# A two-layer network after window attention on one core: its second layer by Strassen's scheme, with decoded weights and activations kept in DRAM

## The chip, the cores and the metric

The kernel runs on one core of a Trainium2 chip. The metric is the device time of one execution in microseconds (us). The core has a matrix engine (PE, also called TensorE; its weight loads are listed as PEld), a vector engine (DVE), a scalar engine (ACT), GpSimd (POOL) and an engine that issues transfers (SP). They share an on-chip memory, SBUF; PE writes its sums to accumulators in PSUM.

## The reference

```python
# q, k, v: (4, 8, 576, 64) fp32; weights fp64
scores = where(0 <= i - j < 64, scale * q @ k.T, -1e9)
attn = softmax(scores)                               # attn @ v: 2304 tokens x 512
x = (attn @ v).transpose(0, 2, 1, 3).reshape(2304, 512)
h = maximum(maximum(x @ w1, x @ w2), x @ w3)         # 512 -> 768
x = h @ w_out                                        # 768 -> 512
h = x @ w_in                                         # 512 -> 2048
g = where(h >= 1, h, where(h <= -1, 0, (h + 1) ** 2 / 4))
out = g @ w_out2                                     # 2048 -> 512
```

## The kernel before

Three pieces of work follow one another and overlap. The attention runs in 36 groups of 64 queries (all 8 heads at once). The first layer runs in 9 blocks of 256 tokens: 18 products (6 tiles of 128 features by 3 weights, `a_item`) whose maximum is taken as they are read out of PSUM, the tiles `ht`, and 4 products back to 512 features (`b_item`). Its results `x2s` go to DRAM (`x2d`). The second layer runs in blocks of 512, 512, 512, 512 and 256 tokens: for each of 16 feature tiles `c_mm` makes the first product, `c_act` the activation and `d_item` the share of the second product, three tiles later.

All products are made in three passes. Each operand is split into a high part (rounded to the type that PE multiplies) and a low part (the rest), and PE adds high by high, high by low and low by high. So a group of 12 matmuls is 4 tiles of the sum by 3 passes. To split costs a copy (`act_copy`, on ACT) and a subtraction (`sub`, on DVE or POOL, line 118).

The weights are fp64. Words of 1024 columns are loaded (`wst`), turned into numbers by two instructions of ACT (lines 181 and 115), a shift and an addition of DVE (lines 188 and 189), and split by ACT and POOL. The 12 pairs of weight tiles of the first layer are decoded during the attention. The 16 pairs of the second layer are decoded in the last block of the first layer and the first block of the second, each right before its first use, and stay in SBUF.

The queries and keys reach their transposed form in two ways. Groups up to `PET` are loaded in whole rows (`nat`) and transposed by PE (`tp`, line 275); the others are loaded by SP in many small pieces (`raw`, line 241), four groups at a time, and transposed by DVE.

The order is written out: each step gets a due time (`put`), steps are sorted by it, and `chained` ties the instructions of PE, ACT and DVE to that order. SP takes its transfers in the order in which the program names them, and waits at one whose buffer is not free. Buffers from one pool with the same tag take turns (`wst`, `raw` and `x2r` share three buffers, `NW`).

Of the kernel before, what the change touches and what calls it, by code (L numbers as in the profile page):

```python
# [21 lines left out]
NW = 3  # L22
# [6 lines left out]
PET = 16  # L29
# [11 lines left out]
DLAG = 3  # L41
# [12 lines left out]
EW = 1  # L54
W2STEP = 3.6
W2LAG = (5.6, 6.4, 8.1, 8.2)
W2IN = 10
# [10 lines left out]
def kernel(ctx, tc, q, k, v, w1, w2, w3, wo1, wi2, wo2, out, x2d):  # L68
# [36 lines left out]
    blocks2 = []  # L105
    t0 = 0
    for n in (512, 512, 512, 512, 256):
        blocks2.append((t0, n))
        t0 += n
    assert t0 == NT  # L110
    N1 = max(n for _, n in blocks1)
    N2 = max(n for _, n in blocks2)
# [35 lines left out]
    wslot = {}  # L148

    def w_load(pair, slot):  # L150
        st = stg.tile([P, 1024, 2], I32, tag="wst", name="wst", bufs=NW)
        for x, (w, f) in enumerate(pair):
# [8 lines left out]
            wslot[w, f] = slot[:, :, 512 * x:512 * x + 512]  # L161
# [44 lines left out]
    pet = range(PET)  # L206
# [8 lines left out]
    def load(g):  # L215
# [49 lines left out]
    def prep(g):  # L265
# [154 lines left out]
    def b_item(j, dt):  # L420
# [7 lines left out]
        st = stg.tile([P, N1], F32, tag="x2s", name="x2s", bufs=2)  # L428
# [296 lines left out]
```

## Time and profile before

| | us |
|---|---|
| median of three runs | 822.22 (821.86 to 822.59) |
| span of the profiled execution | 818.0 |
| profiled execution as a run: span and the 4.2 us around it | 822.2 |
| PE busy | 788.3 |
| DVE busy | 351.2 |
| ACT busy | 338.5 |
| POOL busy | 162.2 |

The profile comes from one execution. Its span runs from the first to the last recorded instruction; the profiled execution has no time of its own beside it, so the median of the runs stands for it. A busy time counts the time in which an engine has at least one instruction under way. For PE the end of a matmul is modelled, so "busy" tells that it had work, and how fast the work went is read from the distance between matmuls. The granted clock (PEclk) is given as a share of PE's full 2.4 GHz; its lower level is 1.2 GHz.

### The profile page before, as it was taken

Reading aid. Unit: us, or ns where it says so; the run is one execution under the profiler, and the core shown is the slowest. Engines: PE = TensorE matmul, PEld = TensorE weight load, DVE = VectorE, ACT = ScalarE, POOL = GpSimd, SP = SyncE. Lnnn points to the kernel's source line nnn. Section 1 sums busy time; section 2 is a strip of 40 time slices with the busy share of each in tenths; the row PEclk is TensorE's granted clock in tenths of the full one; section 3 lists DMA queues with packets and bytes.
Section 4 is the critical chain, followed back from the end, with each engine's and each line's share of the span. In section 5 each row is a group of like instructions: output and inputs, shape, how many; then the busy total and the mean of one; then the engine's idle time right before and its main releaser. Section 6 shows DMA issues by size and latency. Waiting matters only on the chain.

```text
span 818.0 us, 14563 instructions
## 1 busy us (share of the span) xinstructions
PE 788.3 (96%) x5776; PEld 698.5 (85%) x5776; DVE 351.2 (43%) x871; ACT 338.5 (41%) x769; POOL 162.2 (20%) x157
## 2 busy tenths in 40 slices
PE   5798999899999999999899999999999999999997
PEld 4597899799999999999888788888888888888896
DVE  4777333233333333334669935323433334323333
ACT  6897443333333434435597523221331232221232
POOL 2677322212221222313645400000000000000000
PEclk9599999999999999999999999999999999999999
DMA  9995344341421313205555500000010001000100
GB/s 263 259 288 140 76 79 84 61 91 42 92 83 49 86 49 83 77 18 176 166 175 206 180 1 35 17 1 0 1 52 1 0 1 52 0 1 1 51 2 26
DMA packets 127812, 62.69 MB, mean 77 GB/s; under 512 B 98048, under 2 KB 120576, under 8 KB 127744
## 3 DMA queue, kind: packets, MB, share of 16 engines
q1 hardware_dynamic: 122560, 57.04, 25.2%
q10 hardware_dynamic: 5184, 4.72, 1.7%
q8 instruction: 45, 0.74, 0.4%
q14 instruction: 23, 0.19, 0.1%
HBM read 52.30 MB, written 9.44 MB: 75 GB/s over the span
## 4 chain that ended last, share of the span: by engine, by line
PE 82%; SPq 4%; ACT 4%; DVE 2%; POOL 2%; issue 2%; DMA 1%; ACTq 0%; DVEq 0%; POOLq 0%
PE acc L668 25%; PE hp L603 24%; PE ps L403 21%; PE ps L425 7%; SPq L241 4%; PE ops L377 2%; PE pps L356 1%; PE sps L314 1%; POOL u L118 1%; ACT wst L181 1%; ACT sm L337 1%; DVE wt L189 1%; ACT wst L115 1%; ACT u L115 0%; DMA raw<-in_q 0%
## 5 line engine op out<-in xcount | busy, mean ns | idle before, releaser
L403 PE MATMUL ps<-xt,u 128*128 128x256 f32 x1944 | 238.5, 283 | 10.0 <-ACT ht L115 5.2
L403 PEld LDWEIGHTS ps<-xt,u 128*128 128x128 f32 x1944 | 232.8, 191 | 12.7 <-ACT ht L115 5.6
L603 PE MATMUL hp<-x2t,u 128*128 128x512 f32 (+1 forms) x720 | 161.6, 372 | 0.0
L668 PE MATMUL acc<-u,g 128*128 128x512 f32 x648 | 160.4, 396 | 0.0
L648 ACT ACTIVATE u<-hp,half 128x512 f32<-128x512 f32 (+1 forms) x80 | 51.5, 644 | 240.1 <-PE hp L603 240.1
L603 PEld LDWEIGHTS hp<-x2t,u 128*128 128x128 f32 x720 | 126.8, 188 | 27.5 <-DVE gt L651 0.3
L668 PEld LDWEIGHTS acc<-u,g 128*128 128x128 f32 x648 | 120.9, 188 | 28.3
L651 DVE SCALAR_TENSOR_TENSOR gt<-u,hp 128x512 f32<-128x512 f32 (+1 forms) x80 | 50.6, 633 | 153.1 <-ACT u L649 153.0
L412 DVE TENSOR_TENSOR ht<-ps,ht 128x256 f32<-128x256 f32 x108 | 45.4, 421 | 119.4 <-PE ps L403 76.1
L425 PE MATMUL ps<-h,u 128*128 128x256 f32 x648 | 79.4, 280 | 1.7 <-POOL h L118 1.7
L425 PEld LDWEIGHTS ps<-h,u 128*128 128x128 f32 x648 | 76.9, 188 | 3.0 <-POOL h L118 1.9
L118 POOL TENSOR_TENSOR u<-wt,u 128x512 fp32r<-128x512 f32 x48 | 70.9, 1503 | 41.6 <-ACT u L115 41.4
L118 POOL TENSOR_TENSOR h<-ht,h 128x256 fp32r<-128x256 f32 x54 | 43.7, 809 | 117.6 <-ACT h L115 117.5
L347 POOL TENSOR_TENSOR sm<-sm,rs 128x512 f32<-128x512 f32 (+1 forms) x36 | 35.7, 993 | 130.7 <-DVE rs L346 109.7
L115 ACT ACTIVATE h<-ht 128x256 fp32r<-128x256 f32 x54 | 22.5, 417 | 90.6 <-DVE ht L412 90.6
L337 ACT ACTIVATE sm<-sm,nm 128x128 f32<-128x128 f32 (+1 forms) x144 | 55.1, 387 | 6.6 <-DVE nm L325 4.0
L118 DVE TENSOR_TENSOR g<-gt,g 128x512 fp32r<-128x512 f32 (+1 forms) x80 | 56.0, 700 | 2.7
L668 PE MATMUL acc<-v,g 128*128 128x512 f32 x216 | 53.7, 394 | 0.0
L655 DVE CAST g<-gt 128x512 fp32r<-128x512 f32 (+1 forms) x80 | 35.2, 440 | 42.6 <-PE acc L668 39.7
L603 PE MATMUL hp<-x2t,v 128*128 128x512 f32 (+1 forms) x240 | 53.0, 371 | 0.0
L603 PEld LDWEIGHTS hp<-x2t,v 128*128 128x128 f32 x240 | 42.2, 188 | 8.6
L668 PEld LDWEIGHTS acc<-v,g 128*128 128x128 f32 x216 | 40.3, 188 | 8.9
(51 smaller groups left out, 594.6 us busy)
## 6 DMA issues: line engine op xcount, KB each, us to landing
wst<-in_moe_w_out SPq DMA_DIRECT2D x22, 512.0 KB, 4.7
wst<-in_moe_w SPq DMA_DIRECT2D x18, 512.0 KB, 6.8
wst<-in_moe_w_in SPq DMA_DIRECT2D x16, 512.0 KB, 3.8
vr<-in_v SPq DMA_DIRECT2D x24, 256.0 KB, 4.4
x_scratch<-x2s ACTq DMA_DIRECT2D x36, 128.0 KB, 1.8
out<-ob SPq DMA_DIRECT2D x18, 256.0 KB, 2.0
x2r<-x_scratch SPq DMA_DIRECT2D x4, 1024.0 KB, 5.1
vr<-in_v SPq DMA_DIRECT2D x19, 128.0 KB, 3.4
```

The source lines that it names most:

```text
L118: eng.tensor_tensor(dst, a, b, op=ALU.subtract)
L241: nc.sync.dma_start(t[32 * a:32 * a + 32, p, 2 * x:2 * (x + n1), :], src[b1, 2 * p + a // 2, i1 * BL:(i1 + n1) * BL, 32 * (a % 2):32 * (a ...
L337: nc.scalar.activation(sm[:, p, 0:W], sm[:, p, 0:W], AF.Exp, bias=d["nm"][:, p:p + 1], scale=-1.0, accum_out=ss[:, p:p + 1])
L347: nc.gpsimd.tensor_tensor(sm[:, :, 0:W], sm[:, :, 0:W], rs.unsqueeze(2).to_broadcast([P, NP, W]), op=ALU.mult)
L403: nc.tensor.matmul(ps[:, 0:n], w_col((w, f), wl, kt), xt[:, xl, kt, 0:n], start=(x == 0), stop=(x == len(passes) - 1))
L412: nc.vector.tensor_tensor(t[:, 0:n], ps[:, 0:n], part[j, f][:, 0:n], op=ALU.max)
L425: nc.tensor.matmul(ps[:, 0:n], w_col((3, f), wl, dt), hts[j, f][:, xl, 0:n], start=(x == 0), stop=(x == len(passes) - 1))
L603: nc.tensor.matmul(ps[:, 0:n], w_col((4, f), wl, kt), x2t[tb][:, xl, kt, 0:n], start=(x == 0), stop=(x == len(passes) - 1),)
L648: nc.scalar.activation(u[:, 0:n], ps[:, 0:n], AF.Relu, bias=half, scale=2.0 ** (-WS / 2 - 1))
L651: nc.vector.scalar_tensor_tensor(gt[:, 0:n], u[:, 0:n], 2.0 ** WS, ps[:, 0:n], op0=ALU.min, op1=ALU.max)
L655: nc.vector.tensor_copy(g[:, 0, 0:n], gt[:, 0:n])
L668: nc.tensor.matmul(accs[t], g[:, gl, t * P:(t + 1) * P], wslot[5, f][:, wl], start=(f == 0 and x == 0), stop=(f == KF2 - 1 and x == 2),)
```

## The change

**The second layer's two products** use Strassen's scheme (in the form with few additions). Each operand is divided in four quarters; seven sums of quarters on each side are multiplied, and the seven products are added to the four quarters of the result: 7 products in the place of 8. In the first product a unit is a block of 576 tokens (two halves of 288) by a pair of feature tiles (p and p + 8): 7 products of 6 matmuls with 288 columns. There are 32 units. In the second product a chunk is 256 tokens (two halves of 128) by two pairs of feature tiles: 2 x 7 products of 3 matmuls with 256 columns, 36 chunks.

**The sums** cost instructions: `combine` makes each of 4 sums from two operands in SBUF, for x2 on DVE (`x2_steps`), for weights on POOL (`w_steps`), for the activations on DVE (`g_steps`). All seven parts are split into high and low. The results are added from PSUM by DVE (`c_sums`, `c_rest`, `d_out`).

**Two more arrays lie in DRAM.** The decoded weights of the second layer (`td`) are decoded in the first layer, one pair every `W2STEP` steps from block 2 on, stored, and loaded again in the second layer. The activations (`gd`) are stored by the unit and loaded again by the chunk, all first products being made before the second ones.

**The attention's raw loads**: four more groups (16, 17, 26, 27) go through PE, so that 16 groups in four chunks are left for `raw`. Each chunk is 32 transfers in a buffer of its own (128 in all, before 224), due 14.9 steps ahead (`RAWS`, before 21), and `after_queued` fixes where they stand among SP's weight loads.

On PE the second layer was a plain alternation of both products, 12 matmuls each. In the middle of it, before (`hp` is an accumulator of the first product, `acc` one of the second):

```order
L668 MATMUL acc<-u_61,g 128x512 x12
L603 MATMUL hp<-x2t,u_65 128x512 x12
L668 MATMUL acc<-u_62,g 128x512 x12
L603 MATMUL hp<-x2t,u_66 128x512 x12
L668 MATMUL acc<-u_63,g 128x512 x12
L603 MATMUL hp<-x2t,u_67 128x512 x12
L668 MATMUL acc<-u_64,g 128x512 x12
```

Now a unit of the first product is (`ca`, `cb`, `cc`, `ce` are one set of accumulators, `arena` holds sums of weights and tokens)

```order
L728 MATMUL ca_5170<-arena 128x288 x6
L728 MATMUL cb_5171<-arena 128x288 x6
L728 MATMUL cc_5172<-arena 128x288 x6
L728 MATMUL ce_5173<-arena 128x288 x6
L728 MATMUL ca_5170<-arena 128x288 x6
L728 MATMUL cc_5172<-arena 128x288 x6
L728 MATMUL ce_5173<-arena 128x288 x6
```

and the last chunk of the second product (`dy`, `dx`, `dz`, `dw` are its accumulators)

```order
L926 MATMUL dy_7788<-left,arena 128x256 x6
L926 MATMUL dx_7789<-left,arena 128x256 x6
L926 MATMUL dz_7790<-left,arena 128x256 x6
L926 MATMUL dw_7791<-left,arena 128x256 x3
L926 MATMUL dy_7788<-left,arena 128x256 x6
L926 MATMUL dx_7789<-left,arena 128x256 x6
L926 MATMUL dz_7790<-left,arena 128x256 x6
L926 MATMUL dw_7791<-left,arena 128x256 x3
```

The two products have moved apart: all units come first, then all chunks, in matmuls of 288 and 256 columns.

On DVE the work of the second layer before was that of `c_act`, three instructions for a group of 12 matmuls:

```order
L651 SCALAR_TENSOR_TENSOR gt<-u,hp 128x512
L655 CAST g<-gt 128x512
L118 TENSOR_TENSOR g<-gt,g 128x512
L651 SCALAR_TENSOR_TENSOR gt<-u,hp 128x512
L655 CAST g<-gt 128x512
L118 TENSOR_TENSOR g<-gt,g 128x512
```

Now, in two chunks of the second product near its end (`plain` are loaded activations, `evt` the output's sums):

```order
L499 TENSOR_TENSOR plain<-plain 128x256 x4
L115 TENSOR_TENSOR side<-plain,side 128x1024
L938 SCALAR_TENSOR_TENSOR evt<-dy_7788,evt 128x256
L938 SCALAR_TENSOR_TENSOR evt<-dx_7789,evt 128x512
L938 SCALAR_TENSOR_TENSOR evt<-dx_7789,evt 128x256
L938 SCALAR_TENSOR_TENSOR evt<-dz_7790,evt 128x512
L938 SCALAR_TENSOR_TENSOR evt<-dw_7791,evt 128x256
L499 TENSOR_TENSOR plain<-plain 128x256 x4
L115 TENSOR_TENSOR arena<-plain,arena 128x1024
```

The activation has moved to the first product's units; beside the second product stand sums and splits with both operands in SBUF, and between them the sums of the outputs from PSUM.

On SP, in the first layer around the second chunk of raw loads, before:

```order
L241 DMA raw<-in_q 32x8x32 x16
L241 DMA raw<-in_k 32x8x32 x8
L259 DMA vr<-in_v 128x8x64 x2
L241 DMA raw<-in_k 32x8x32 x8
L241 DMA raw<-in_q 32x6x32 x16
L241 DMA raw<-in_q 32x2x32 x13
```

and now (`t_scratch` is the array of decoded weights, `wst` the next weights' words):

```order
L281 DMA vr<-in_v 64x8x64
L283 DMA vr<-in_v 128x8x64
L564 DMA t_scratch<-wt 128x1024
L165 DMA wst<-in_moe_w_in 128x4x256 x2
L266 DMA raw<-in_q 32x8x32 x16
L266 DMA raw<-in_k 32x8x32 x16
L564 DMA t_scratch<-wt 128x1024
```

The pieces of one chunk have become 32 equal ones, and loads and stores of the second layer's weights have come to stand ahead of them and behind.

The core of the difference (the bodies that it replaces stand in the kernel above):

```diff
-PET = 16
+PET = (*range(18), 26, 27)
...
-DLAG = 3
+RAWS = -14.9
...
-EW = 1
-W2STEP = 3.6
-W2LAG = (5.6, 6.4, 8.1, 8.2)
-W2IN = 10
+W2AT = 2
+W2STEP = 8.5
+W2LAG = 5.2
+W2EVERY = 1.2
...
-    blocks2 = []
-    t0 = 0
-    for n in (512, 512, 512, 512, 256):
-        blocks2.append((t0, n))
-        t0 += n
...
+    NH = 288
+    NB2 = NT // (2 * NH)
+    NPR = KF2 // 2
...
+    def after_queued(fn, *args):
+        with ExitStack() as stack:
+            for i in queued:
+                stack.enter_context(tc.issue_after(i))
+            n = len(nc.cur_bb.bb.instructions)
+            fn(*args)
+        ends = [i for i in nc.cur_bb.bb.instructions[n:] if i.engine == mybir.EngineType.SP]
+        queued[:] = ends[-1:] or queued
...
-        if g not in pet and (g - PET) % CH == 0:
...
+        if g in raws[::CH]:
+            after_queued(raw_load, g)
+    def raw_load(g):
+        raw = apool.tile([P, 2, NP, 2 * CH, 32], F32, tag="raw", name="raw", bufs=1)
+        for y, (nm, src) in enumerate((("q", q), ("k", k))):
...
+    PASSES = ((0, 0), (0, 1), (1, 0))
...
+    def sums(x, role):
+        x = [x[:, i] for i in range(7)]
+        if role is RA:
+            return (
+                (x[4], x[2], x[3], ALU.add), (x[2], x[0], x[2], ALU.subtract),
+                (x[5], x[4], x[0], ALU.subtract), (x[6], x[1], x[5], ALU.subtract),
+            )
+        return (
+            (x[4], x[3], x[1], ALU.subtract), (x[1], x[1], x[0], ALU.subtract),
+            (x[5], x[3], x[1], ALU.subtract), (x[6], x[2], x[5], ALU.subtract),
+        )
+    def combine(eng, x, role, i):
+        o, a, b, op = sums(x, role)[i]
+        eng.tensor_tensor(o, a, b, op=op)
+    def low(eng, o, x, hi):
+        sub(eng, o, x, f32(hi))
...
+    def x2_steps(b, y):
+        c, x = x2c[b], plain["x", b, y]
+        steps = [(combine, (nc.vector, x, RB, i)) for i in range(4)]
+        for r in (slice(0, 4), slice(4, 7)):
+            hi, lo = (o[:, r, y] for o in c.hl)
+            steps += [(act_copy, (hi, x[:, r])), (low, (nc.vector, lo, x[:, r], hi))]
+        if b < 2:
...
+    def t_load(n):
+        t = staging(("t", n), 256)
+        nc.sync.dma_start(t[:, 0:4], td[n].rearrange("p (s c) -> p s c", s=4))
+    def w_steps(n, c, shared=False):
+        x, role = plain["t", n], c.role
+        steps = [(combine, (nc.gpsimd, x, role, i)) for i in range(4)]
+        steps += [(act_copy, (c.hl[0][:, r], x[:, r])) for r in (slice(0, 4), slice(4, 7))]
+        if shared:
+            steps.append((low, (nc.vector, c.hl[1][:, 0:4], x[:, 0:4], c.hl[0][:, 0:4])))
+        for i in range(4 if shared else 0, 7):
+            steps.append((low, (nc.gpsimd, c.hl[1][:, i], x[:, i], c.hl[0][:, i])))
+        return steps
...
+    def w2_decode(n, x):
+        st = w2st[n]
+        if x < 2:
+            w_word(st, 1 - x)
+        elif x == 2:
+            w_shift(st)
+        else:
+            w_add(st, slice(512 * (x - 3), 512 * (x - 2)))
+    def w2_store(n):
+        nc.sync.dma_start(td[n], decoded.pop(id(w2st[n])).bitcast(F32))
...
-            w_split(U[n // 2], w_load(order1[n:n + 2], U[n // 2]))
+            st = []
+            after_queued(lambda: st.append(w_load(order1[n:n + 2], U[n // 2])))
+            w_split(U[n // 2], st[0])
...
+            put(vq + (LP if g in pet else RAWS), load, g)
...
+    for n in range(2 * NPR):
+        at = begin[W2AT] + W2STEP * n
+        put(at, w2_load, n)
+        for x in range(5):
+            put(at + W2LAG + W2EVERY * x, w2_decode, n, x)
+        put(at + W2LAG + W2EVERY * 4 + 0.5, w2_store, n)
...
+    x2_at(put, turn + 0.3, 3.2, 0.5, 0)
+    wt_at(put, turn + 0.4, turn + 3.0, 0.5, 0, wc, 0)
+    x2_at(put, turn + 14.2, 3.0, 0.5, 1)
+    wt_at(put, turn + 18.2, turn + 20.6, 0.55, 1, wc, 1)
...
+    def product(o, m, wt, wx, start):
+        passes = [(kt, wl, xl) for kt in range(2) for wl, xl in PASSES]
...
+                o, wt.of(m, wl)[:, kt * P:(kt + 1) * P], wx.of(m, xl)[:, kt], start=start and x == 0, stop=x == len(passes) - 1, skip_group_check=True,
...
+    def c_mm(s, m):
+        b, p = UNITS[s]
+        a, u, c, d = banks[s % 2]
+        o = {1: a, 2: a, 6: u, 5: c, 3: c, 7: d, 4: d}[m]
+        product(o[:, 0:NH], m, wc[p], x2c[b], m in FIRST)
...
+    UNITS = [
...
+    def c_copy(s):
+        act_copy(ev[s % 2][0], banks[s % 2][0][:, 0:NH])
+    def c_sums(s, x):
+        two, h, u = ev[s % 2]
+        a, six, c, d = banks[s % 2]
+        o, y, z = ((two, six, two), (h[:, 2], c, two), (h[:, 2], d, h[:, 2]))[x]
+        add(o, y[:, 0:NH], z)
+    def c_relu(s, first):
+        two, h, u = ev[s % 2]
+        o, x = (u[:, 0], banks[s % 2][0][:, 0:NH]) if first else (u[:, 1:4], h)
+        nc.scalar.activation(o, x, AF.Relu, bias=half, scale=2.0 ** (-WS / 2 - 1))
+        nc.scalar.activation(o, o, AF.Square)
+    def c_rest(s, x):
+        two, h, u = ev[s % 2]
+        add(h[:, x], banks[s % 2][2 + x][:, 0:NH], two)
+    def c_last(s, first):
+        two, h, u = ev[s % 2]
+        o, x = (u[:, 0], banks[s % 2][0][:, 0:NH]) if first else (u[:, 1:4], h)
+        nc.vector.scalar_tensor_tensor(o, o, 2.0 ** WS, x, op0=ALU.min, op1=ALU.max)
+    def c_store(s):
+        b, p = UNITS[s]
+        t0, u = b * 2 * NH, ev[s % 2][2]
+        for i in range(2):
+            nc.sync.dma_start(
+                gd[p + NPR * i, :, t0:t0 + 2 * NH].rearrange("p (c n) -> p c n", c=2), u[:, 2 * i:2 * i + 2]
+            )
...
+    for s in range(len(UNITS)):
+        for x, m in enumerate(FIRST if s else ()):
+            put2(0.0 if (s, m) == (1, 6) else s + x / 7, c_mm, s, m)
+        put2(s + 0.16 if s else -1.0, c_copy, s)
+        for x, at in enumerate((0.3, 0.45, 0.56)):
+            put2(s + at, c_sums, s, x)
+        for x, m in enumerate((2, 3, 4)):
+            put2(s + (x + 4) / 7, c_mm, s, m)
+        put2(s + 0.72, c_relu, s, True)
+        put2(s + 0.9, c_last, s, True)
+        put2(s + 0.89, c_rest, s, 0)
+        put2(s + 1.0, c_rest, s, 1)
+        put2(s + 1.17, c_relu, s, False)
+        put2(s + 1.66, c_last, s, False)
+        put2(s + 1.8, c_store, s)
...
+    def g_load(k):
+        t0, t = k // 4 * 256, staging(("g", k), 256)
+        for i in range(2):
+            for j in range(2):
+                f = NPR * j + 2 * (k % 4)
+                nc.sync.dma_start(
+                    t[:, 2 * i + j].rearrange("p (r t) -> p r t", r=2),
+                    gd[f:f + 2, :, t0 + P * i:t0 + P * (i + 1)].rearrange("f p n -> p f n"),
...
+    def g_steps(k):
+        c, x = gc[k % 4], plain["g", k]
+        steps = [(combine, (nc.gpsimd if k == 1 else nc.vector, x, RA, i)) for i in range(4)]
+        x = x.rearrange("p s (r t) -> p s r t", r=2)
+        for r in (slice(0, 4), slice(4, 7)):
+            hi, lo = (o[:, r] for o in c.hl)
+            eng = nc.gpsimd if (k < 1 or k > 4) and r.stop == 7 else nc.vector
+            steps += [(act_copy, (hi, x[:, r])), (low, (eng, lo, x[:, r], hi))]
+        return steps
...
+    def d_mm(k, r, m):
+        tb, c = divmod(k, 4)
+        y, x, z, w = dsets[tb % 2]
+        p = 2 * c + r
+        o, first = {1: (y[:, 0], 1), 6: (y[:, 1], 0), 5: (x[:, 0], 1), 7: (x[:, 1], 0), 2: (z[:, 0], 1),
+                    3: (z[:, 1], 0), 4: (w[:, 0], 1)}[m]
+        for i, (gl, wl) in enumerate(PASSES):
+            nc.tensor.matmul(
+                o, gc[k % 4].of(m, gl)[:, r], wd[p].of(m, wl),
+                start=bool(first and p == 0 and i == 0), stop=p == NPR - 1 and i == 2, skip_group_check=True,
...
+        if n == 0:
+            act_copy(m[:, 0], y[:, 0], scale=s)
+        elif n < 6:
+            mad(*(
+                (two, y[:, 1], m[:, 0]), (m[:, 1:3], x, two.unsqueeze(1).to_broadcast([P, 2, 256])),
+                (o[:, 3], x[:, 0], m[:, 2]), (o[:, 0:2], z, m[:, 0:2]), (o[:, 2], w[:, 0], m[:, 2]),
+            )[n - 1])
+        else:
...
```

## Rows read from the trace of the kernel before

**Rows 1.** The page: busy time, share of the span and instructions of each engine.
```profile
PE 788.3 (96%) x5776; PEld 698.5 (85%) x5776; DVE 351.2 (43%) x871; ACT 338.5 (41%) x769; POOL 162.2 (20%) x157
```

**Rows 2.** Windows: us, busy PE PEld DVE ACT POOL, PEclk, DMA share, GB/s.
```profile
149.00:152.00 3.00, 1.80 (x8) 1.80 (x9) 1.43 (x8) 3.00 (x15) 0.51 (x1) 0.61 0.38 70
...
300.00:350.00 50.00, 50.00 (x540) 48.73 (x539) 15.15 (x61) 21.49 (x64) 11.04 (x12) 1.00 0.30 86
...
360.00:455.00 95.00, 92.41 (x622) 83.52 (x621) 63.48 (x72) 65.36 (x88) 44.63 (x34) 1.00 0.49 166
...
600.00:650.00 50.00, 50.00 (x217) 40.38 (x216) 16.37 (x28) 11.87 (x18) 0.00 (x0) 1.00 0.03 11
```

**Rows 3.** The chain that ended last: start us, us, what.
```profile
112.06 0.87 PE tp L275 x8
...
347.56 15.40 PE ps L403 x132
...
364.04 10.00 PE ps L403 x84
...
374.04 6.32 PE ps L425 x54
...
625.79 2.79 PE hp L603 x12
...
628.58 2.81 PE acc L668 x12
...
803.82 1.44 PE hp L603 x12
...
808.07 5.61 PE acc L668 x24
```

**Rows 4.** Timelines at PE's gaps: start us, us, instruction, idle before and releaser.
```profile
128.06 14.37 SPq L241 DMA_DIRECT2D raw<-in_q  x29
...
148.03 1.08 ACT L115 ACTIVATE pt<-pps 128x512 f32<-128x512 f32 x2 [5.60 <-DMA raw<-in_q]
...
150.20 12.75 PE L403 MATMUL ps<-xt,u 128*128 128x256 f32 x96 [3.99 <-ACT ht L115]
...
390.31 1.92 PE L403 MATMUL ps<-xt,u 128*128 128x256 f32 x14 [0.88 <-DVE ht L412]
...
406.96 2.26 PE L425 MATMUL ps<-h,u 128*128 128x256 f32 x17 [1.71 <-POOL h L118]
```

**Rows 5.** Groups by form: line engine op names shapes xcount | busy, mean ns | idle before.
```profile
L118 POOL TENSOR_TENSOR u<-wt,u 128x512 fp32r<-128x512 f32 x48 | 70.9, 1503 | 41.6 <-ACT u L115 41.4
...
L118 POOL TENSOR_TENSOR h<-ht,h 128x256 fp32r<-128x256 f32 x54 | 43.7, 809 | 117.6 <-ACT h L115 117.5
...
L189 DVE CUSTOM_DVE_ANT_0 wt<-wst,wt 128x2048 uint16<-128x2048 uint16 x28 | 41.3, 1476 | 3.4 <-ACT wst L115 1.9
...
L181 ACT ACTIVATE wst<-wst 128x1024 f32<-128x1024 f32 x28 | 32.0, 1142 | 8.0 <-DMA wst<-in_moe_w_out 4.7 <-DMA wst<-in_moe_w 2.1 <-ACT x2s L115 1.2
...
L188 DVE TENSOR_SCALAR wt<-wst 128x1024 int32<-128x1024 int32 x28 | 29.7, 1062 | 28.3 <-ACT wst L181 12.1 <-DMA x_scratch<-x2s 9.2 <-POOL u L118 2.9
...
L118 DVE TENSOR_TENSOR g<-gt,g 128x256 fp32r<-128x256 f32 x16 | 6.8, 426 | 0.5
```

**Rows 6.** Timelines of DVE and POOL side by side, columns as in Rows 4.
```profile
392.01 3.01 POOL L118 TENSOR_TENSOR v<-wt,v 128x512 fp32r<-128x512 f32 x2 [0.43 <-ACT v L115]
...
392.03 0.42 DVE L412 TENSOR_TENSOR ht<-ps,ht 128x256 f32<-128x256 f32 x1 [0.59 <-PE ps L403]
...
423.32 0.69 DVE L118 TENSOR_TENSOR g<-gt,g 128x512 fp32r<-128x512 f32 x1
...
424.81 3.13 POOL L118 TENSOR_TENSOR u<-wt,u 128x512 fp32r<-128x512 f32 x2 [3.67 <-ACT u L115]
...
425.10 1.68 DVE L118 TENSOR_TENSOR g<-gt,g 128x512 fp32r<-128x512 f32 x1
...
426.70 1.79 DVE L188 TENSOR_SCALAR wt<-wst 128x1024 int32<-128x1024 int32 x1
```

More of the change, by code (lines that the diff above doesn't have):

```diff
@@ L67, with kernel @@
 @with_exitstack
-def kernel(ctx, tc, q, k, v, w1, w2, w3, wo1, wi2, wo2, out, x2d):
+def kernel(ctx, tc, q, k, v, w1, w2, w3, wo1, wi2, wo2, out, x2d, td, gd):
     nc = tc.nc
@@ L205 @@
     chunk = {}
-    pet = range(PET)
+    pet = set(PET)
+    raws = [g for g in range(NG) if g not in pet]
     def blk(g):
@@ new lines, in x2_steps @@
+    def x2_steps(b, y):
[6 more added lines that the diff above has]
+            return steps
+        hi, lo = (o[:, :, y] for o in c.hl)
+        steps = [*steps[:4], steps[4], steps[6]]
+        return steps + [(low, (nc.gpsimd, lo[:, i], x[:, i], hi[:, i])) for i in range(7)]
@@ L608 @@
+    assert sorted(UNITS) == [(b, p) for b in range(NB2) for p in range(NPR)]
     order.sort(key=lambda e: e[:2])
@@ L698 @@
-    for x in range(len(seq) - DLAG, len(seq)):
-        d_item(*seq[x])
+            side = p2.tile([P, XN + WN], F32R, name="side")
+            x2c[0] = region(side, 0, (2, NH), RB)
+            x2c[1] = region(arena, 0, (2, NH), RB)
+            wc[0] = region(side, XN, (256,), RA)
+            for p in range(1, 5):
+                wc[p] = region(arena, XN + WN * (p - 1), (256,), RA)
+            pc0_stack, pc1_stack = ExitStack(), ExitStack()
+            pc0 = pc0_stack.enter_context(tc.tile_pool(name="pc0", bufs=1, space=PSUM, reuse_waits="tile"))
@@ new lines, with add @@
+    left = lp.tile([P, WN // 2 + 2 * WN], F32R, name="left")
+    evt = lp.tile([P, 2, 8, NH], F32, name="evt")
+    wc[5] = Combos(area(arena, XN + 4 * WN, (256,)), area(left, 0, (256,)), RA)
+    wc[6], wc[7] = (region(left, WN // 2 + WN * x, (256,), RA) for x in range(2))
+    ev = [(evt[:, x, 0], evt[:, x, 1:4], evt[:, x, 4:8]) for x in range(2)]
+    def add(o, a, b):
+        nc.vector.tensor_tensor(o, a, b, op=ALU.add)
+    def c_copy(s):
+        act_copy(ev[s % 2][0], banks[s % 2][0][:, 0:NH])
@@ new lines, in steps_at, with wt2 @@
+    def steps_at(places, make, *args):
+        for x, at in enumerate(places):
+            put2(at, lambda x=x: (lambda s: s[0](*s[1]))(make(*args)[x]))
+    def wt2(load, at, his, n, into, p, low=None):
+        put2(load, t_load, n)
+        lows = [his[1] + 0.01 * x for x in range(1, 8)]
+        if low:
+            lows[:4] = [low]
+        steps_at((*(at + 0.01 * x for x in range(4)), *his, *lows), lambda: w_steps(n, into[p], bool(low)))
+    for p, at, his in ((2, -0.4, (0.57, 0.88)), (3, 1.3, (1.88, 2.56)), (4, 2.9, (3.56, 3.88)), (5, 4.5, (5.56, 5.88)),
+                       (6, 6.1, (6.88, 7.56)), (7, 7.7, (8.56, 8.88))):
+        wt2(at - 0.9, at, his, p, wc, p)
@@ new lines, with d_open @@
+    CU = (2 * 21 * 256) / (42 * 288.0)
+    end = float(len(UNITS))
+    dsets = {}
+    def d_open():
+        pc1_stack.close()
+        pc0_stack.close()
+        pd = ctx.enter_context(tc.tile_pool(name="pd", bufs=1, space=PSUM, reuse_waits="tile"))
+        for x in range(2):
+            dsets[x] = [pd.tile([P, 2, 256], F32, name=f"{y}{x}") for y in ("dy", "dx", "dz", "dw")]
+    def d_mm(k, r, m):
[8 more added lines that the diff above has]
+                start=bool(first and p == 0 and i == 0), stop=p == NPR - 1 and i == 2, skip_group_check=True,
+            )
```

288 lines of the change are left out of this document (162 added, 126 removed).

## The prediction

> **What bounds the kernel now.** First the page's line of busy times [rows 1]: PE is busy in 788.3 of 818.0 us, DVE in 351.2, ACT in 338.5 and POOL in 162.2. Then the busy times by stage [rows 2]: in 50 us of the first layer and in 50 us of the second PE is busy throughout at the full granted clock of 2.4 GHz, while no other engine exceeds 21.5 us. So what counts is how long PE's matmuls take, and whether an engine, with less work for PE to hide behind, is late. The chain of waits [rows 3] gives PE's pace: 12 matmuls of 512 columns in 2.79 to 2.81 us (0.2333 us each), 24 of 512 at the end in 5.61 (0.234), 12 of 256 columns in 1.44 (0.12; some rows 1.43, 0.1192), 132 of 256 columns in 15.40 (0.1167), 84 in 10.00 (0.119). Last the timelines of the few places where PE stands [rows 4]: 3.99 us before 150.20, 0.88 before 390.31 and 1.71 before 406.96.
>
> The span is 818.0 us and the median of the runs 822.2; the 4.2 us between them lie outside the span and stay. I sum against 822.2.
>
> **Second layer's matmuls.** Removed: 64 groups of 12 at 512 columns and 16 groups of 12 at 256 in the first product, 864 matmuls of 512 (72 groups of 12) in the second. By [rows 3]: 64 x 2.80 + 16 x 1.44 + 72 x 2.80 = 403.8 us. Added: 32 units (8 pairs of feature tiles by 4 token blocks of 576) x 7 x 6 = 1344 matmuls of 288 columns, and 36 chunks (256 tokens, two pairs) x 2 x 7 x 3 = 1512 of 256. The 256-column ones cost 0.1192 as in the second layer's last block, together 180.2. The trace has no 288: the line through 0.1192 (256) and 0.2333 (512) is 0.000446 us per column, which gives 0.1335 and 179.4 in all. New total 359.6, so **-44**. With the first layer's 0.1167 for 256 columns (and 0.1313 for 288) it would be 352.9, that is -51; the price of 84 in 10.00 gives the same as mine. If each product lost some 0.02 us where a new accumulator begins (224 + 504 of them), 15 us would come back; no row shows such a loss, as the groups of 54 in 6.32 us [rows 3] run at 0.117 across three accumulators. I keep -43 to -51.
>
> **Transposes on PE.** Four more groups of queries come through PE: two pairs with 8 transposes each, 16 x 0.109 us from 0.87 for 8 [rows 3]: **+1.7** (0 to +2).
>
> **The stall at 146 to 150 us.** In [rows 4] ACT waits 5.60 us for a transfer of raw queries, 29 of whose issues hold SP for 14.37 us (0.496 each); the eviction ht behind that wait on ACT is what PE waits for, 3.99 us. Then the clock: the windows [rows 2] show 0.61 of full in 149 to 152, so it had fallen to 1.2 GHz for part of it, after PE's stand; the 96 matmuls from 150.20 took 12.75 instead of 96 x 0.1167 = 11.20. After the change SP issues 128 raw loads instead of 224, in four chunks of 32, each with a buffer of its own and ordered among the weight loads (the order of SP above). 32 x 0.496 = 15.9 us of issue must fit into the 14.9 steps of 1.4 us, 20.9 us, by which they are due ahead, which leaves 5. I take all of it as gone: **-5.4** (0 if a chunk is late again, where the next visit's transposes wait). The new stores of decoded weights wait on SP for DVE's addition; queued behind them are values, weights' words and these raw loads, so a late addition of some us would eat the 5.
>
> **Decoding moved into the first layer.** 16 pairs of weight tiles are decoded either way. What moves is their place: before, most of it lay between 360 and 420 us; now each 8.5 steps of the first layer take 2 ACT instructions of 1.14 us, one DVE shift of 1.06 and two halves of the 1.48 add [rows 5], 2 loads and 1 store. On ACT that is 2.3 us and on DVE 2.5 in 8.5 x 1.4 = 12 us of PE (12 matmuls per step by the 0.1167 pace), where both engines have half of the time free [rows 2]. An eviction ht queued behind such a 1.14 us instruction comes late; PE has three accumulators, so two of 1.40 us each are its cover. What the trace shows where cover fails is the 0.88 us at 390.31. 16 times that is 14; never is 0. I take **+2**, nearer to 0, since before, pairs decoded every 3.6 steps (denser than the 8.5 now) beside the last block's matmuls left PE busy for 92.41 of the 95 us from 360 on [rows 2], with those two gaps alone. The two gaps there (0.88 and 1.71) get new ones in their place, as reload and splitting of the first weights and activations come at the same turn: net 0 (-2.6 to +5).
>
> **First product beside its helpers.** PE takes 42 x 0.1335 = 5.6 us per unit. ACT: 5 instructions over 2592 columns, by 11.87 us for 18 of mostly 512 columns [rows 2] about 3.3 us, and by the same pace 2.3 for the 1792 columns of a weight's high parts. DVE: five of 288 columns at 0.46 and one of 864 at 1.05 (0.426 for 256 [rows 5], 0.69 for 512 alone [rows 6], so 0.00103 per column): 3.4 to 3.8 us. POOL: 11 of 256 columns at 0.81 [rows 5], 8.9 us per weight, one in 1.6 units (9.0 us). All fit, though DVE has also to prepare x2 in units 9 to 16. On SP a unit's stores wait for its activation, and reloaded weights and x2 queue behind them; these are due a unit or more ahead. **+3** for single late steps (0 to +10).
>
> **Second product beside its helpers.** PE takes 42 x 0.1192 = 5.0 us per chunk. DVE takes 4 x 0.43 for the sums, 1.22 for one split of 1024 columns, and a quarter of the outputs' 2.66 (3 x 0.43 and 2 x 0.69): 3.6 us. POOL splits 768 columns: 2.2 us by the 0.81 for 256 and 1.50 for 512 [rows 5], which hold waits themselves, so 1.9 to 2.2. They look independent, but [rows 6] shows otherwise: the split g of 512 columns, 0.69 us at 423.32, took 1.68 at 425.10 with POOL busy from 424.81 on; the shift L188 at 426.70 took 1.79, against its mean of 1.06 [rows 5]. The addition ht (one operand in PSUM) at 392.03 took its 0.42 beside POOL from 392.01. So instructions of DVE that read and write SBUF alone wait for POOL's; those that read PSUM do not. Sums and splits are of the first kind, outputs of the second: 1.72 + 1.22 + 2.0 = 4.9 us in a row, just below PE's 5.0, and 5.6 to 5.8 if everything lies in a row. I take **+4** for 36 chunks; bounds 0 and 31 x 0.8 = 25.
>
> [...]
>
> **Tail.** The last 24 matmuls end at 813.7 [rows 3], and 4.3 us of output follow; now one addition of the last of four results and its transfer follow: 0 (-1 to +2).
>
> **Sum.** 822.2 - 44 + 1.7 - 5.4 + 2 + 0 + 3 + 4 + 0 = **783.5 us**.
>
> **The rivals.** (A) DVE and POOL set the pace of the second product: 5.8 us per chunk against PE's 5.0. For it the 1.68 and 1.79 of [rows 6]; against it that outputs do not wait. 25 in place of 4: about 804. [...] (B) The first layer pays for the decoding each time: 14 in place of 2, about 795. Against it the long stretches at full PE in [rows 2] with half of ACT free. (C) All is hidden and 256 columns run at 0.1167: -51 in place of -44 and 4 of the 9 us of losses gone, about 772. (D) The other side: if DVE's additions that read PSUM wait for POOL as well, 6 per unit plus 2 sums at some 0.6 us each make DVE 3.8 + 4.8 = 8.6 us in the units beside POOL's weights, 3 us over PE's 5.6; POOL works at 14 weights in this layer, 6 of them with 7 instructions in place of 11, 8 x 8.9 + 6 x 5.7 = 105 us or 19 units, so +57 in place of 3, about 837. It decides from 39 / 68 = 0.57 us lost per unit and chunk. The 0.42 us of ht beside POOL speaks against it. (E) The change doesn't do what it says, since a matmul of half the columns costs as much as a whole: [rows 3] excludes it for 256 columns (1.44 for 12).
>
> **How the numbers follow.** My forecast 58% (own range 776 to 790), A 18%, B 10%, C 9%, D 4%, E 1%. The range 772 to 803 leaves out half of C, half of A, D and E: 18%. What a measurement of this kernel can tell from no change is 0.2%, 1.6 us. Forecast, A, B and C are all faster: 95%; D and E slower, 4%; 1% ends between.
>
> **What would show it.** In the chain after the change, 42 matmuls of 288 columns should take 5.6 us, 42 of 256 5.0, with PE busy about 746 us; no idle PE of several us near 146; the windows of the second product with PE near 95%. The steps are wrong where PE stands in the second product behind DVE's split or POOL's (A), where ht's eviction waits behind L181's like in the first layer (B), or where additions that read PSUM take over 0.8 us beside POOL (D).

## The result, and the profile after

The changed kernel takes 789.96 us (median of four runs, 788.42 to 794.41) against 822.04 of before: a ratio of 0.9616 (0.9585 to 0.9646), 32 us less. The forecast was 783.5, with 772 to 803 as its range: the direction, the range and the size hold; 6.5 us of the gain are missing.

The page's busy times after the change answer to [rows 1]:

```profile
PE 751.0 (95%) x6824; PEld 729.8 (93%) x6824; DVE 506.3 (64%) x1107; ACT 423.5 (54%) x855; POOL 347.6 (44%) x341
```

PE has 37 us less to do and DVE 155 us more, POOL more than twice as much. The windows (columns as in [rows 2]) show where:

```profile
149.00:152.00 3.00, 3.00 (x28) 3.00 (x27) 1.79 (x6) 1.58 (x5) 1.30 (x2) 1.00 0.00 0
...
300.00:350.00 50.00, 49.29 (x530) 47.80 (x529) 21.73 (x71) 25.21 (x68) 11.95 (x14) 1.00 0.57 181
...
360.00:455.00 95.00, 91.38 (x749) 89.85 (x749) 54.95 (x91) 51.23 (x83) 64.68 (x79) 1.00 0.31 103
...
480.00:530.00 50.00, 49.98 (x377) 49.75 (x377) 37.09 (x70) 37.47 (x56) 38.55 (x43) 1.00 0.40 141
...
650.00:750.00 100.00, 99.00 (x831) 98.27 (x830) 89.18 (x124) 37.17 (x45) 41.62 (x20) 1.00 0.45 132
```

PE runs through at 149 to 152 us, where it had been slow after a stand. In the second product DVE is busy for 89 of 100 us, close behind PE. PE's pace, from its timeline (the first matmuls of two units, then of two chunks) and, for the first layer, from the chain, answers to [rows 3]:

```profile
484.17 0.43 PE L728 MATMUL ca<-arena 128*128 128x288 f32 x2
...
489.69 0.96 PE L728 MATMUL ca<-arena,left 128*128 128x288 f32 x6
...
740.42 0.88 PE L926 MATMUL dy<-side 128*128 128x256 f32 x6
...
745.40 0.87 PE L926 MATMUL dy<-arena,side 128*128 128x256 f32 x6
```
```profile
142.62 15.40 PE ps L427 x132
```

A unit of 42 matmuls takes 5.52 us here (the median of all units is 5.58, 0.133 per matmul) and a chunk 4.98 (0.1186). The first layer's 132 matmuls take their 15.40 as before. Of the losses, one chain answers to [rows 4]. Its rows are of SP, ACT and PE in the first product:

```profile
407.81 15.59 SPq L536 DMA_DIRECT2D plain<-t_scratch  x3
...
423.45 2.88 SPq L830 DMA_DIRECT2D g_scratch<-evt  x4
...
427.88 0.50 ACT L814 ACTIVATE evt<-ca,half 128x288 f32<-128x288 f32 x1 [5.16 <-DMA g_scratch<-evt]
...
429.20 1.07 PE L728 MATMUL ca<-arena 128*128 128x288 f32 x6 [1.58 <-ACT evt L112]
```

SP stands within three loads of weights until 423.45, as no staging buffer is free. Behind them wait the stores of two units' activations; ACT can't write the next activation over them for 5.16 us, ACT's copy of a sum stands behind that, and PE waits for the copy: 2.5 us with what follows, and 1.7 once more at unit 5. The second product, DVE, POOL and PE side by side, answers to [rows 6]:

```profile
729.10 3.32 DVE L499 TENSOR_TENSOR plain<-plain 128x256 f32<-128x256 f32 x4
...
746.39 1.67 DVE L499 TENSOR_TENSOR plain<-plain 128x256 f32<-128x256 f32 x4
```
```profile
728.73 2.15 POOL L115 TENSOR_TENSOR arena<-plain,arena 128x768 fp32r<-128x768 f32 x1 [3.55 <-ACT arena L112]
```
```profile
730.93 0.38 PE L926 MATMUL dy<-arena 128*128 128x256 f32 x1 [0.35 <-POOL arena L115]
```

Four sums take 1.67 us where POOL is idle and 3.32 where it works. With the outputs of every fourth chunk on top, a split comes late and PE loses 0.6 us.

### The profile page after: what moved, and what is told of

It is laid out like the page before. It is cut to its first block, busy times and chain, and to the rows that moved or that the text cites. A ratio compares the mean times of both kernels' runs of the same rounds, so it can differ in the third digit from the quotient of the medians.

```text
span 787.5 us, 17772 instructions
## 1 busy us (share of the span) xinstructions
PE 751.0 (95%) x6824; PEld 729.8 (93%) x6824; DVE 506.3 (64%) x1107; ACT 423.5 (54%) x855; POOL 347.6 (44%) x341
## 4 chain that ended last, share of the span: by engine, by line
PE 55%; issue 15%; POOL 13%; DMA 4%; ACT 4%; DVE 3%; SPq 1%; ACTq 0%; DVEq 0%; POOLq 0%
PE ps L427 24%; PE ps L449 8%; POOL arena L115 6%; PE cc L728 5%; PE ce L728 5%; PE ca L728 5%; POOL side L115 4%; PE cb L728 2%; POOL left L115 2%; PE ops L401 2%; PE sps L338 1%; PE pps L380 1%; DMA g_scratch<-evt 1%; POOL plain L499 1%; DMA t_scratch<-wt 1%
## 5 line engine op out<-in xcount | busy, mean ns | idle before, releaser
L427 PE MATMUL ps<-xt,arena 128*128 128x256 f32 x1944 | 238.7, 283 | 7.0 <-ACT xt L112 2.8
L427 PEld LDWEIGHTS ps<-xt,arena 128*128 128x128 f32 x1944 | 232.7, 190 | 9.9 <-ACT ht L112 3.3
L499 DVE TENSOR_TENSOR plain<-plain 128x256 f32<-128x256 f32 (+1 forms) x172 | 115.7, 690 | 6.0 <-DMA plain<-g_scratch 3.0
L115 POOL TENSOR_TENSOR arena<-plain,arena 128x256 fp32r<-128x256 f32 (+2 forms) x70 | 83.4, 1216 | 62.8 <-ACT arena L112 54.5
L112 ACT ACTIVATE arena<-plain 128x1024 fp32r<-128x1024 f32 (+1 forms) x64 | 59.5, 956 | 67.9 <-DVE plain L499 33.3
L115 POOL TENSOR_TENSOR side<-plain,side 128x768 fp32r<-128x768 f32 (+2 forms) x40 | 57.4, 1457 | 72.4 <-ACT side L112 54.0
L449 PE MATMUL ps<-h,arena 128*128 128x256 f32 x648 | 79.5, 280 | 0.0
L449 PEld LDWEIGHTS ps<-h,arena 128*128 128x128 f32 x648 | 76.9, 188 | 1.0 <-issue 1.0
L499 POOL TENSOR_TENSOR plain<-plain 128x256 f32<-128x256 f32 x68 | 59.0, 874 | 35.3 <-DMA plain<-t_scratch 21.9
L209 DVE CUSTOM_DVE_ANT_0 wt<-wst,wt 128x1024 uint16<-128x1024 uint16 (+1 forms) x44 | 45.7, 1046 | 2.9 <-ACT wst L112 1.8
```

The costliest lines, as they stand in the source:

```text
L112: nc.scalar.activation(dst, src, AF.Copy, scale=scale)
L115: eng.tensor_tensor(dst, a, b, op=ALU.subtract)
L209: nc.vector.tensor_tensor(t[:, x], t[:, x], st[:, x, 0], op=ALU.add)
L427: nc.tensor.matmul(ps[:, 0:n], w_col((w, f), wl, kt), xt[:, xl, kt, 0:n], start=(x == 0), stop=(x == len(passes) - 1))
L449: nc.tensor.matmul(ps[:, 0:n], w_col((3, f), wl, dt), hts[j, f][:, xl, 0:n], start=(x == 0), stop=(x == len(passes) - 1))
L499: eng.tensor_tensor(o, a, b, op=op)
```

## The experiments

All ratios are to the kernel before, run beside each on the same chip, with 95% intervals.

| run | ratio | interval | median us |
|---|---|---|---|
| again (the changed kernel) | 0.9623 | 0.9595 to 0.965 | 791.09 |
| store_act | 0.9626 | 0.9602 to 0.965 | 791.75 |
| split_dve | 0.9564 | 0.9538 to 0.9591 | 785.73 |
| no_decode | 0.998 | 0.9962 to 0.9997 | 820.85 |
| sp_order | 0.9652 | 0.9627 to 0.9677 | 793.76 |
| pool_idle | 0.9867 | 0.9843 to 0.9891 | 811.08 |
| no_decode_paced | 0.9592 | 0.957 to 0.9613 | 789.22 |
| eighth | 0.9901 | 0.9878 to 0.9925 | 814.11 |
| joined | 0.9546 | 0.9528 to 0.9564 | 785.08 |
| x2_pool | 0.9751 | 0.9729 to 0.9773 | 800.9 |
| first_units | 0.9559 | 0.9534 to 0.9584 | 784.59 |

**again.** 

> The changed kernel once more, as the measure for the other three of this call. Expected ratio to before 0.9616 (0.9585 to 0.9646), some 790 us. It tells how far two series of one kernel lie apart; a difference of less than that between the others tells nothing.

It came out as expected, 0.9623. Its six runs lie between 786.91 and 794.77 us, and the first layer ends between 408.5 and 412.7 us in the profiles of the nine kernels that do not change it. So losses are compared by stage, in one profile of each kernel, and a "loss" below is the time of a unit over 5.58 us or of a chunk over 4.98.

**Does PE set the pace? eighth.**

```diff
         product(o[:, 0:NH], m, wc[p], x2c[b], m in FIRST)
+        if m == 4:
+            product(o[:, 0:NH], m, wc[p], x2c[b], False)
```

> In each unit of the first product the last product is made twice (6 more matmuls of 288 columns, added to the same accumulator), so 8 products in place of 7; nothing else changes. Theory (PE sets the pace of the first product, 0.1325 us per matmul): 192 x 0.1325 = 25.4 us more, less the some 5 us of stalls that the longer units hide: 810 to 816 us. Rival (the helpers set the pace, so that the seventh product's end was already waiting): less than 13 us more.

23.0 us more than again. A unit takes 6.38 us in place of 5.58 (48 matmuls at 0.133), 25.6 us for 32 units, and the losses at units 3 and 5 shrink to 0.3 and 0.1 us. But unit 9 takes 10.71 us: loads of x2 now stand ahead of stores on SP, and ACT waits for a store:

```profile
467.06 0.50 ACT L816 ACTIVATE evt<-ca,half 128x288 f32<-128x288 f32 x1 [3.70 <-DMA g_scratch<-evt]
```

So each product left out is worth its matmuls' time, less what PE then waits for.

**Is it POOL that holds DVE? split_dve and pool_idle.**

```diff
-            eng = nc.gpsimd if (k < 1 or k > 4) and r.stop == 7 else nc.vector
+            eng = nc.gpsimd if k < 1 and r.stop == 7 else nc.vector
```

> In the second product DVE makes the split of 768 columns that POOL made from chunk 5 on; POOL then has nothing to do there. Theory: DVE's four sums take 3.32 us in place of 1.7 because the last two wait for POOL's instruction, so POOL's split costs DVE as much as it would cost to make it itself (1.0 us alone); DVE then needs 4.6 us per chunk under PE's 4.92, and the losses of 0.6 us at every fourth chunk and 1.9 us at chunk 34 go: 3 to 5 us less. Rival: DVE is the tight engine by its own work, not by the wait; with 1 us more per chunk it comes to 5.0 to 5.6 with its waits for ACT and sets the pace: 3 to 20 us slower.

5.4 us less than again. The window and DVE's timeline in this run:

```profile
650.00:750.00 100.00, 100.00 (x847) 100.00 (x846) 88.57 (x154) 39.39 (x48) 0.00 (x0) 1.00 0.47 138
```
```profile
729.79 1.67 DVE L499 TENSOR_TENSOR plain<-plain 128x256 f32<-128x256 f32 x4
731.92 2.09 DVE L115 TENSOR_TENSOR side<-plain,side 128x1024 fp32r<-128x1024 f32 x2 [0.46 <-ACT side L112]
```

DVE does one instruction more per chunk and is busy no longer (88.57 for 89.18 us), as its sums take 1.67 us again; PE stands nowhere in these 100 us. From chunk 5 on the loss falls from 4.4 (after) and 6.1 us (again) to 0.0. pool_idle adds to split_dve two instructions of POOL per chunk, for whose result nobody waits:

```diff
+        y = f32(hi[:, 4:7]).rearrange("p s r t -> p (s r t)")
+        for i in range(2):
+            z = y[:, 384 * i:384 * (i + 1)]
+            nc.gpsimd.tensor_tensor(arena[:, 24192:24576], z, z, op=ALU.subtract)
```

> DVE makes the split of 768 columns, as in split_dve, and POOL besides subtracts the same number of columns (two instructions of 384) for nobody: nothing waits for its result. Theory (DVE's instructions with two operands in SBUF wait while POOL works, whatever POOL makes): DVE needs its 4.6 us and up to 2 us of waiting per chunk, more than PE's 4.92, over 31 chunks: 20 to 50 us slower than split_dve, 805 to 835 us. Rival (DVE was late only because it waited for POOL's results or buffers): as fast as split_dve, 784 to 788.

25.4 us more than split_dve. DVE and POOL side by side:

```profile
728.97 2.30 DVE L499 TENSOR_TENSOR plain<-plain 128x256 f32<-128x256 f32 x4
731.73 2.73 DVE L115 TENSOR_TENSOR side<-plain,side 128x1024 fp32r<-128x1024 f32 x2 [0.46 <-ACT side L112]
734.38 2.30 DVE L499 TENSOR_TENSOR plain<-plain 128x256 f32<-128x256 f32 x4
```
```profile
732.57 2.57 POOL L914 TENSOR_TENSOR arena<-side 128x384 fp32r<-128x384 f32 x2 [2.84 <-ACT side L112]
```

The sums take 2.30 for 1.67 us and the splits 2.73 for 2.09, and the chunk 5.41 (728.97 to 734.38) for 4.98. DVE waits for POOL though it needs nothing of POOL's: none of DVE's waits from 650 us on is put down to POOL, and the time lies within its instructions. Most of the 25 us are lost at every fourth chunk, which DVE prepares behind the outputs (most of these take 7.1 to 8.8 us in place of 5.04). The additions that read PSUM do not: in the first product the sums from `ce` take 456 ns in the mean of 64, beside a POOL that is busy 77% of the time (38.55 of 50 us at 480):

```profile
L800 DVE TENSOR_TENSOR evt<-ce,evt 128x288 f32<-128x288 f32 x64 | 29.2, 456 | 6.8 <-PE ce L728 5.1
```

**What does decoding cost the first layer? no_decode and no_decode_paced.** In both `w2_decode` is cut; in the second DVE's shift stays, at the place of the last step:

```diff
+        if x == 4:
+            t = decoded[id(st)] = stg2.tile([P, 1024], I32, tag="wt", name="wt", bufs=WT)
+            nc.vector.tensor_scalar(t, st[:, :, 1], 31, None, op0=ALU.logical_shift_left)
```

> The decoding of the second layer's weights in the first layer is left out (two instructions of ACT and three of DVE for each of 16 pairs; a finite part of SBUF is stored in its place); loads and stores stay. Theory: the first layer has room for it, 0 to 2 us less. Rival B of the prediction: decoding delays evictions, up to the 5 us in which PE stands in the first layer after 60 us would go, and with the half clock at 70 us up to 7.

Some 30 us more, which neither theory had. The window from 60 to 145 us, in this run and in the changed kernel:

```profile
60.00:145.00 85.00, 51.73 (x468) 48.81 (x468) 29.00 (x87) 38.12 (x91) 25.35 (x23) 0.78 0.94 275
```
```profile
60.00:145.00 85.00, 81.89 (x854) 78.56 (x855) 37.01 (x133) 45.73 (x126) 31.66 (x30) 0.98 0.59 154
```

With no decoding to hold the buffers, the second layer's words were fetched at once: the DMA engines are busy 94% of the time, the first layer's own words come late, and PE works for 52 of 85 us, at 0.78 of its clock. The run tells what the decoding's pace protects, not what its work costs.

> The decoding is left out (ACT's two instructions and DVE's addition; DVE's shift stays and makes zeros, which are stored and used as the second layer's weights), but the loaded words stay in their buffers until the shift, so that loads and stores come at the pace of the changed kernel. Theory: ACT and DVE have room for the decoding, and the gaps near 227 and 311 us come from transfers; the first layer ends 0 to 2 us earlier than the 410 to 413 us of the changed kernel. Rival B: it ends 4 to 7 us earlier. The first attempt without the decoding could not tell, since the loads then ran ahead of the pace and took the transfers' time from the first layer's own.

The first layer ends at 410.4 us, inside the 408.5 to 412.7 of the runs with the decoding. Its work costs nothing that can be measured; rival B falls. The gap at 227 us is gone in this run, but one of 2.3 us stands at 306.

**Can the losses of the first product be had back? store_act, sp_order, joined, first_units.** store_act has `nc.scalar` for `nc.sync` in `c_store`.

> The two stores of a unit's activations are issued by ACT in place of SP. Theory: in the first product PE lost 2.5 us at unit 3 and 1.7 us at unit 5 because SP stood 15.6 us at loads of weights whose staging buffer was not free, with the stores behind them, and ACT could not write the activation's buffer again; with stores on ACT both losses go, and some of the 5.5 us at the turn to the second product, where the loads of chunk 3 stood behind the last unit's store: 4 to 7 us less, 783 to 786 us. Rival: the losses come from POOL and DVE being late with sums and splits; then they stay, and the two issues of 0.4 us and their waits on ACT make it 0 to 3 us slower.

No gain. Units 3 and 5 lose nothing, so the stores behind the loads were the cause there. But PE now waits 0.4 to 0.6 us at four other places, and 0.93 in place of 0.45 at a fifth, for DVE's sums. Two of them in PE's timeline:

```profile
465.17 0.53 PE L728 MATMUL cc<-side,arena 128*128 128x288 f32 x2 [0.56 <-DVE evt L800]
...
471.50 1.06 PE L728 MATMUL cc<-arena 128*128 128x288 f32 x6 [0.49 <-DVE evt L800]
```

The losses of units 1 to 31 sum to 7.0 us, in again to 7.7. sp_order keeps the stores on SP and fixes SP's order:

```diff
+        if fn in (t_load, x2_load, c_store, g_load):
+            chained(after_queued, fn, *args)
```

> In the second layer SP's transfers keep their due order (stores of a unit ahead of weight loads that are due later), as raw loads do in the first; no transfer is moved to another engine. Theory: the losses of 2.5 us at unit 3 and 1.7 us at unit 5 come from one weight load standing ahead of two units' stores on SP and go now without new ones, since ACT gets no work (stores on ACT removed these two and put four of 0.4 to 0.9 in their place); chunk 3's loads go out together, so some of the 1.4 us at the turn: 4 to 6 us less than the changed kernel, ratio 0.955 to 0.958. Rival: ACT and POOL are late by their own work there, and the loss turns up one unit later: ratio 0.960 to 0.964.

No gain either. Units 3 and 5 lose nothing; at unit 30 the same wait appears, longer, PE standing 6.6 us (SP, then ACT):

```profile
571.10 6.80 SPq L536 DMA_DIRECT2D plain<-t_scratch  x2
```
```profile
582.46 0.50 ACT L814 ACTIVATE evt<-ca,half 128x288 f32<-128x288 f32 x1 [8.13 <-DMA g_scratch<-evt]
```

joined is split_dve, this order with `and (at < 10 or at > 31.8)`, and `30.01` moved to `30.25` for weight pair 5:

> Three edits together: DVE makes the split of 768 columns (split_dve); SP keeps its due order in units 0 to 9 and from the last unit on, but not between, where sp_order lost 6.6 us at unit 30; the high part of one weight pair stands behind ACT's copy of unit 30 in place of ahead of it, where ACT waited 3.1 us for POOL's sums. Theory: 5.4 us less than the changed kernel by the first, 4 by units 3 and 5, 1.7 by unit 30, 0 to 2 at the turn: 778 to 782 us, ratio 0.947 to 0.952. Rival: the losses between units move on to the next tight place, as with stores on ACT and with sp_order: as split_dve, 784 to 787, ratio 0.955 to 0.958.

The rival holds: 785.08 us lies in its 784 to 787, and 0.9546 is not told apart from split_dve's 0.9564. A load of x2 now stands ahead of two stores near unit 10:

```profile
458.51 7.23 SPq L517 DMA_DIRECT2D plain<-x_scratch  x2
465.80 5.53 SPq L830 DMA_DIRECT2D g_scratch<-evt  x4
```
```profile
472.71 0.50 ACT L814 ACTIVATE evt<-ca,half 128x288 f32<-128x288 f32 x1 [4.85 <-PE cc L728]
```

The profile puts ACT's wait down to a product of PE; but the stores went out only from 465.80 to 471.33, and in first_units ACT's wait near that unit is put down to such a store.

first_units is split_dve with the due order for `at < 7` alone:

> split_dve, and SP keeps its due order in units 0 to 6 alone; in the run joined a load of x2 with no free buffer stood 7.2 us ahead of two stores near unit 10 because the due order reached to unit 9, and took 2.9 us back. Theory: units 3 and 5 lose nothing and no other unit more than in split_dve: 4 us less than split_dve, 780 to 783 us, ratio 0.949 to 0.953. Rival: the losses move once more: ratio 0.954 to 0.958.

The rival again: units 3 and 5 lose nothing, one near 477 us loses 1.65 (PE's timeline), and the time is that of split_dve:

```profile
477.95 1.06 PE L728 MATMUL cc<-side,left 128*128 128x288 f32 x6 [1.65 <-DVE evt L800]
```

Three staging buffers serve weights, x2 and activations, and each load that goes out early takes a place in SP's queue ahead of a store. Which unit pays changes with the order; that somebody pays did not, in four tries: units 1 to 31 lose 7.0 us in store_act, 10.7 in sp_order, 6.3 in joined and 6.8 in first_units, for 7.7 in again and 7.8 in split_dve.

**Is ACT's store of x2 the cause of the first layer's gaps? x2_pool** has `nc.gpsimd.dma_start` for `nc.scalar.dma_start` there.

> As split_dve, and the stores of x2 in the first layer are issued by POOL in place of ACT. Theory: near 227 and 311 us ACT is held at the issue of such a store while SP issues raw loads or weight loads, and evictions wait behind it; with POOL as the issuer these gaps of 1.2 to 2.6 us, and the half clock that can follow, go, 2 to 5 us less than split_dve, 781 to 784. Rival: the gaps come from the raw loads' data or from SP's order; they stay, and POOL's work for the issues delays the splits of h (0.82 us, 6 per block): 0 to 10 us slower than split_dve.

15 us more than split_dve. The gap at 227 us is gone (one of 1.35 stands at 312), but ACT waits for the stores' buffers later in the layer, and PE with it:

```profile
389.94 2.93 PE L427 MATMUL ps<-xt,arena 128*128 128x256 f32 x12 [4.67 <-ACT x2s L112]
```

So the issue on ACT has a part in the gap at 227 us, and POOL is the worse issuer. What would remove the gap at no cost was not found.

## Why the prediction was right, and where its sizes were off

**Matmuls.** 32 x 5.58 + 36 x 4.98 = 357.8 us for the forecast 359.6; the line through 256 and 512 columns gave 0.1335 for 288, measured 0.133. The old matmuls had taken 402.8 us in the profile for the 403.8 summed, so the term is -45.0 for -44. eighth confirms the step behind it.

**First layer.** It ends at 410.0 us for 413.6; with the second layer's matmuls that lie before these ends (2.8 us before, 3.2 now) that is -4.1, forecast -1.7 (1.7 - 5.4 + 2). The stand at 146 us is gone, and so are the gaps of 0.88 and 1.71 us at the end of the layer, which the prediction had kept at net 0. Part of the first comes back at another chunk of raw loads (SP, ACT, PE):

```profile
214.68 11.48 SPq L266 DMA_DIRECT2D raw<-in_q  x16
```
```profile
223.28 0.39 ACT L112 ACTIVATE x2s<-ps 128x256 f32<-128x256 f32 x1
226.37 0.33 ACTq L454 DMA_DIRECT2D x_scratch<-x2s  x1
226.74 1.08 ACT L112 ACTIVATE pt<-pps 128x512 f32<-128x512 f32 x2 [3.08 <-DMA raw<-in_q]
```
```profile
228.91 3.30 PE L427 MATMUL ps<-xt,arena 128*128 128x256 f32 x26 [1.47 <-ACT ht L112]
```

The mechanism is the one of [rows 4]: ACT's issue of an x2 store comes 2.7 us after its data, and the profile puts the wait down to a raw load in both kernels (3.08 us here, 5.60 before). The trace's semaphores tell why. All transfers of the program, on SP and ACT alike, take eight landing semaphores in turn, and 531 of the 545 that find one used before wait for it ahead of their issue. The store at 226.37 waits for the one that it will raise itself; the last to raise it was a raw load that SP issued at 224.23 and that landed at 226.01. So such a store waits for a raw load that stands ahead of it in the turn, and the 5 us of room ahead of the transposes, which I had counted, do not bear on that wait. An order in which no such store follows raw loads was not tried. The +2 for decoding was 0.

**First product.** Forecast +3, measured 8.4 us (0.8 in unit 0, 7.6 in the others). This is one of the two terms that were mis-sized: I had written that reloaded weights and x2 queue behind a unit's stores and are due early enough; the profile shows the reverse, stores behind loads that wait for a buffer. That is 4.2 us, at units 3 and 5. Another 2.2 are lost at unit 30, where ACT's copy stands behind the high part of a weight for which POOL's sums are late:

```profile
583.58 1.06 ACT L112 ACTIVATE arena<-plain 128x1024 fp32r<-128x1024 f32 x1 [3.07 <-POOL plain L499]
```

joined took this loss away (unit 30 at 5.56 us), and the next unit lost 1.8. The prediction also counted five additions of 288 columns per unit on DVE; there are six, which gives the upper of its two values, 3.8 us.

**Second product.** Forecast +4, measured 9.9: 4.4 (6.1 in again) from the shared work of DVE and POOL from chunk 5 on, as the prediction's paragraph had it (4.9 us in a row just below 5.0), and 5.5 in the first five chunks, which no term held. In these the last weights' splits on POOL, the chunks' own splits and the last unit's activation on DVE meet (the last took 1.61 us for 1.05), and PE's stands are followed by a stretch at half the granted clock, 1.2 GHz, six matmuls in 1.28 us (613.72 to 615.00) for 0.71:

```profile
606.66 1.61 DVE L824 SCALAR_TENSOR_TENSOR evt<-evt 128x864 f32<-128x864 f32 x1
```
```profile
613.00:616.00 3.00, 2.83 (x13) 2.66 (x13) 2.50 (x6) 1.69 (x2) 0.00 (x0) 0.50 0.89 249
```
```profile
611.21 0.50 PE L926 MATMUL dy<-left,arena 128*128 128x256 f32 x2 [1.41 <-ACT arena L112]
...
613.72 1.48 PE L926 MATMUL dx<-left,arena 128*128 128x256 f32 x6
...
615.00 1.45 PE L926 MATMUL dz<-left,arena 128*128 128x256 f32 x6
```

This account of the turn is read from the rows; no run took the loss away or tested it.

The Trainium skill, "SBUF — State Buffer", section "Who interferes with whom", states that a DVE instruction with two SBUF inputs contends with a GpSimd instruction that reads SBUF, and that one with at most one SBUF input, outside the 2-port perf modes, does not. pool_idle agrees with the first half (sums of 2.30 for 1.67 us), and the sums from `ce`, with one input in PSUM, agree with the second (456 ns beside a busy POOL).

**The base.** I took 4.2 us outside the span. The runs list both: 789.31 for a span of 787.5, and for before 822.35 for 820.6, so 1.8. The profiled execution of before was thus some 2.4 us quicker than the median, and its rows were a little better than the time they were summed against.

**Together.** Against the forecast, span to span: -1.0 (matmuls), -2.4 (first layer), +5.4 (first product), +5.9 (second product) and +0.3 (tail) give +8.2, as measured (787.5 for 783.5 - 4.2); the base takes 2.4 of that back, less the 0.7 by which the median lies over this run, and 6.5 are left. So the path and its main term, the matmuls, were right, and the losses were forecast at 7 us and came to 18; that the time still lies close to the forecast owes something to the matmuls, the first layer and the base, which erred the other way. Rival A was a true mechanism at a fifth of its price, B and D fell; C's pace of 0.1167 was not reached (0.1186), and the helpers were not hidden.

**A version that beats both** is split_dve, with joined and first_units equal to it: 785 us, a ratio of 0.955 to 0.956.

## What to carry to other kernels

When a scheme trades PE's work for sums, count for DVE and POOL together every instruction that reads and writes SBUF alone; if the sum comes near PE's pace, giving POOL's share to DVE can cost nothing. On a queue that takes transfers in order, look for loads that wait for a buffer with stores behind them, and give the loads a later place only after counting who uses the buffers, since moving the order alone moved the loss. A transfer that work paces is also held back by that work: leave the work out and the transfers run ahead of the ones that are needed first.

## What was not expected of the hardware

In pool_idle two instructions of 384 columns on POOL took 2.57 us beside DVE and cost DVE 1.27 us, less than POOL's time: one by one, DVE's split at 722.07 took 1.58 us behind POOL's first (721.77 to 722.84), POOL's second, at 722.91, took 1.42 behind that split, and DVE's next sum, at 723.57, took 1.04 for 0.42 behind POOL's second. The two engines take turns by the instruction there, and the wait is one instruction's rest and not all of POOL's work. And the late x2 stores on ACT, which look like an engine held back while SP issues many small transfers, are a wait of the program for a raw load's landing.
